# A decode block on one core: the q projection with a head's weights stationary, in a loop of 32 turns

## The chip, the cores and the metric

The kernel runs on one core of a Trainium2 chip. The metric is device time in microseconds (us), the median of repeated runs. A profile of one execution shows, for each engine, when each instruction ran and what released it. PE is the matrix engine (PEld its weight loads, PEq or PEldq the instructions of its sequencer: registers, branches), DVE the vector engine, ACT the scalar engine, POOL a fourth engine that only prepares constants here, and SP the engine whose queue issues nearly all DMA transfers.

## What is computed

One decode step of a transformer block for four sequences: layer norm, attention over a cache of 8192 positions with 32 heads of 128, output projection, residual, layer norm, a gated MLP, residual. All inputs are bf16.

```python
# x: 4 x 1 x 512; k_cache, v_cache: 4 x 32 x 8192 x 128; wq: 512 x 4096; wo: 4096 x 512
q = (layernorm(x) @ wq).reshape(B, Sq, H, Dh).transpose(0, 2, 1, 3)
scores = einsum("bhqd,bhkd->bhqk", q, k_cache) * (Dh ** -0.5)
o = einsum("bhqk,bhkd->bhqd", softmax(scores), v_cache)
h = x + o.transpose(0, 2, 1, 3).reshape(B, Sq, H * Dh) @ wo
g, u = layernorm(h) @ w_gate, layernorm(h) @ w_up       # 512 x 1792 each
return h + (sigmoid(g) * u) @ w_down
```

The query is one row for each sequence, so q is a product of a 4 x 512 matrix with a 512 x 4096 one: small work beside the caches, of which every byte is read once (some 537 MB of the 551 MB that the kernel reads).

## The kernel before

**Units.** The 4 x 32 pairs of sequence and head are worked in 32 units of 4 heads (`NU = 32`, `HU = 4`). A unit's K is one transfer of 8 MB into one of two slots of the tile `KV` (slot 0 for even units, slot 1 for odd), its V one of 8 MB into slot 2. The weights `wq` (4 MB) are loaded first, into slot 2 too, so V of unit 0 can't be issued before the q projection has read them.

**The DMA queue.** SP issues every large transfer in one fixed order: wq, then K0, K1, V0, K2, V1, K3, V2, and so on (lines 532 to 542; the list `order`, line 225). The first three go out at once. V0 waits for `t_qp`, the last product of the q projection (line 535). After that K of unit u waits for the last transposition of unit u-2 (`t_kd`, a small memset on DVE in line 361), and V of unit u waits for the product that reads the last of V of unit u-1 (`t_vd`, line 419). An issue that waits holds back all issues behind it on SP.

**A unit.** `unit(u)` emits, on PE and DVE: `scores(u)`, 16 chunks, for each a DVE block transposition of K (line 335) and four PE products against the queries (line 344; a loop of 8 turns on PE, two chunks a turn); `maxima(u)` on DVE and the exponential on ACT; the query tile of the next unit (`q_window`, line 328); `pv(u - 1)`, 64 products of the previous unit's weights with its V (line 405), the scaling copy on ACT (line 410) and four small products (line 415); and `weights(u)`, four DVE transpositions of the exponentials (line 375). Between units 1 and 31 PE runs one loop turn a unit, DVE and ACT one loop turn for two units.

**The q projection.** After the layer norm of x (lines 273 to 287), 32 products (line 301) run in two groups of 16, one for each half of the 4096 columns: the stationary operand is a column group of the normalised x (128 x 4), the moving one 512 columns of wq, four products side by side in the array. DVE turns each group's result by blocks (line 308), and a cast (line 309) picks the bf16 queries out of the turned tile `qt` into `q_all`. Then `q_window(0)` (line 328) makes unit 0's query tile, and only behind it on DVE stands the first transposition of K0.

```python
t_qp = emit("pe", f, [t_wq, t_xn, t_ps0, t_selc], incs=4)
...
w = t_qp if n == 2 else None          # n counts the transfers of K and V: n == 2 is V0
```

Of the kernel before, what the change touches and what calls it, by code (L numbers as in the profile page):

```python
# [18 lines left out]
class _Prog:  # L19
# [52 lines left out]
    def emit(self, eng, fn, waits=(), incs=1, ch=None):  # L72
        todo = self._waits(eng, waits)
        key = ch or eng
        tok = self.token(key, incs) if incs else None
        self._put(eng, todo, key, fn, incs, 1)
        return tok
# [41 lines left out]
def bass_sequential_preLN__mha_block_cached__glu_gated_glu__decode_kernel(  # L119
# [12 lines left out]
    B, _sq, D = A_x.shape  # L132
    _, H, S, DH = A_k_cache.shape
    F = B_w_gate.shape[1]
    assert DH == 128 and H == 32 and D == 512 and F % 128 == 0 and B == 4 and S == 8192
    NC = D // 128
    NFT = F // 128
    FG = F // 4
    HU = 4
    NU = B * H // HU  # L140
    R = S // 32
    SLOT = R * DH
    NSL = 3
# [10 lines left out]
    prog = _Prog({"p2d": "dve", "d2d": "dve", "a2d": "dve", "d2p": "pe", "a2p": "pe",  # L154
                  "d2a": "act", "p2a": "act",
                  "k0": "dve", "k1": "dve", "v2": "pe"})
    emit = prog.emit

    with ExitStack() as es:
        def SB(name, shape, dt):  # L160
            return es.enter_context(nc.sbuf_tensor(name, shape, dt))

        def raw(t):
            return t.tensor if hasattr(t, "tensor") else t

        kT = SB("kT", [128, 2 * TW], FP32)
# [3 lines left out]
        q_all = SB("q_all", [128, NU, 4], BF16)  # L170
        spare = SB("spare", [128, 24], FP32)
        KV = SB("KV", [128, NSL * SLOT], BF16)
# [21 lines left out]
        agg = kT[0:B, TW + 264:TW + 266]  # L194
        std = kT[0:B, TW + 268:TW + 270]
        xnT = hnT = kTb[:, 2 * (TW + 288):2 * (TW + 288) + NC * B]
        qt = kT[:, 0:4 * NU // B * 32]
        h_sb = kT[0:B, TW + 512:TW + 512 + D]

        def reg(slot, off, size):  # L200
            return KV[:, slot * SLOT + off:slot * SLOT + off + size]

        wq_v = reg(2, 0, NC * H * DH).rearrange("p (c f) -> p c f", c=NC)
        x_bf = reg(2, 24 * 1024, D)[0:B, :]
        wo_v = reg(1, 0, WOJ * D).rearrange("p (j f) -> p j f", j=WOJ)
        wg_v = reg(1, 16384, NC * F).rearrange("p (c f) -> p c f", c=NC)
        wu_v = reg(1, 16384 + NC * F, NC * F).rearrange("p (c f) -> p c f", c=NC)
        wd_v = reg(2, 0, NFT * D).rearrange("p (t f) -> p t f", t=NFT)
# [6 lines left out]
        PS = es.enter_context(nc.psum_tensor("PS", [128, 4096], FP32))  # L215
        bank = [PS[:, 512 * i:512 * (i + 1)] for i in range(8)]
        SBK, OBK, EX, XS, XO, QB, DN = 0, 1, 2, 3, 4, (5, 6), 7
# [10 lines left out]
        t_wq = prog.token("wq", 16)  # L228
# [22 lines left out]
        for j in range(4):  # L251
# [9 lines left out]
        t_selc = emit("pool", lambda e: e.affine_select(  # L261
            out=hw4, in_=hw4, compare_op=ALU.is_ge, fill=0.0, base=31,
            pattern=[[0, 8], [32, 4], [0, 4]], channel_multiplier=-1), [t0])
        emit("pool", lambda e: e.memset(part[:, :], 1.0))
        t_pool = emit("pool", lambda e: e.memset(PTz[:, :], 0.0))
        for b in (OBK, EX, *QB, DN):
            t_ps0 = emit("act", lambda e, b=b: e.activation(bank[b], bass.AP(raw(Lq), 0, [[528, 128], [0, 512]]), ACT.Copy), [t_lq0])

        def cols(t, c):
            return t[:, c:c + NC * (B - 1) + 1:NC]  # L270

        def layernorm(src, waits, dst):
            a = emit("dve", lambda e: e.bn_stats(bst, src), waits)
            a = emit("dve", lambda e: e.bn_aggr(agg, bst), [a])
            a = emit("act", lambda e: e.activation(std[:, 0:1], agg[:, 1:2], ACT.Sqrt, bias=eps[0:B, :]), [a, t_eps])
            a = emit("dve", lambda e: e.reciprocal(std[:, 1:2], std[:, 0:1]), [a])
            t_row = emit("dve", lambda e: e.tensor_scalar(
                row, src, agg[:, 0:1], std[:, 1:2], op0=ALU.subtract, op1=ALU.mult), [a])

            def f(e):  # L280
                ins = None
                for c in range(NC):
                    ins = e.matmul(cols(bank[XS], c), row[:, c:c + NC * 127 + 1:NC], ident[0:B, 0:B],
                                   start=(c == 0), stop=(c == NC - 1), skip_group_check=True)
                return ins
            a = emit("pe", f, [t_row, t_ident])
            return t_row, emit("dve", lambda e: e.tensor_copy(dst, bank[XS][:, 0:NC * B]), [a])
# [3 lines left out]
             [t_x, t_ident])  # L291
        _, t_xn = layernorm(x_bf, [t_x], xnT)

        t_qr = []
        for g in range(2):
            def f(e, g=g):
                made = []
                for c in range(NC):
                    for h in range(HU):
                        rhs = wq_v[:, c, 2048 * g:2048 * (g + 1)].rearrange("p (k h d) -> p h k d", k=4, h=HU)[:, h]  # L300
                        made.append(e.matmul(PS[32 * h:32 * h + B, 512 * QB[g]:512 * QB[g] + 512], cols(xnT, c), rhs,  # L301
                                             start=(c == 0), stop=(c == NC - 1), tile_position=(0, 32 * h)))
                return made[-4:]
            t_qp = emit("pe", f, [t_wq, t_xn, t_ps0, t_selc], incs=4)

            src = bank[QB[g]].rearrange("p (k w r) -> p r k w", k=8, r=2)
            dst = qt[:, 512 * g:512 * (g + 1)].rearrange("p (k r w) -> p r k w", k=8, r=2)
            t_qr.append(emit("dve", lambda e, src=src, dst=dst: e.transpose(dst, src), [t_qp]))
        t_q = emit("dve", lambda e: e.tensor_copy(
            q_all[:, :, :].rearrange("p (b g) t -> p g b t", b=B),  # L310
            qt.rearrange("p (g t w) -> p g w t", t=4, g=NU // B)[:, :, 0:B, :]), t_qr)

        t_tr, t_sc, t_pv, t_ex, t_mx, t_exp, t_ptz, t_lq, t_ocp, t_rs, t_kd, t_vd, t_sum = ({} for _ in range(13))
        TU = 2
# [107 lines left out]
        def unit(u, t=0):  # L422
# [6 lines left out]
            if u:  # L429
# [4 lines left out]
                                      skip_group_check=True), [t_pool, t_ps0], incs=0)  # L434
# [4 lines left out]
        for u in range(1, NU):  # L439
            t, first = divmod(u - 1, TU)  # L440
            if u == NU - 1:
                prog.close("dve", "act")
                t = 0
# [90 lines left out]
        for n, (x, u) in enumerate(order):  # L534
            w = t_qp if n == 2 else None
            if n >= 3:
                w = t_kd[u - 2] if x == "k" else t_kd[NU - 2] if u == NU - 1 else t_vd[u - 1]
            slot = slots[x, u]
            cache = A_v_cache if x == "v" else A_k_cache
            src = cache[u // (NU // B), HU * (u % (NU // B)):HU * (u % (NU // B) + 1), :, :].rearrange("h (p r) d -> (h p) (r d)", p=32)  # L540
# [51 lines left out]
```

## Time and profile before

| | us |
|---|---|
| median of three timed runs | 1277.33 (1277.13 to 1277.39) |
| span of the profiled execution | 1275.6 |
| what the timed median has over that span | 1.7 |
| PE busy, DVE busy, ACT busy in the span | 779.7, 762.3, 59.0 |
| the q projection on PE (line 301) | 13.00 to 16.59 |
| first transposition of K0 on DVE (line 335) | 32.27 |

The profiled execution has no time of its own beside its span; the span runs from its first instruction to its last, and the 1.7 us over it in the timed runs is what lies around. A row of the profile's timeline gives the start, the duration, the engine and line, what was written from what, and in brackets how long the engine had been idle before and what ended that. A chain that ended last is followed back from the last instruction; a row of it names who held up the end. Rows of PEldq are the sequencer's own instructions.

### The profile page before, as it was taken

What the parts mean: (1) busy time and instruction counts of PE and PEld (TensorE: products, weight loads), DVE (VectorE), ACT (ScalarE), POOL (GpSimd) and SP (SyncE); (2) the same over time, 40 slices, a digit from 0 to 9 for tenths busy, and PEclk for the clock granted to TensorE, in tenths of its full rate; (3) what the DMA queues carried; (4) which work ended last, traced back from release to release, by engine and by line L of the source; (5) the groups of instructions that cost most, each with busy time, mean ns of one, the idle gap of its engine ahead of it and who ended that gap; (6) DMA issues with size and microseconds to landing.
All of it is one profiled execution on the core that took longest, in us unless ns stands there. A gap on an engine that the chain in (4) does not pass through costs nothing.

```text
span 1275.6 us, 14073 instructions
## 1 busy us (share of the span) xinstructions
PE 779.7 (61%) x4588; PEld 328.5 (26%) x4636; DVE 762.3 (60%) x917; ACT 59.0 (5%) x114; POOL 5.7 (0%) x22
## 2 busy tenths in 40 slices
PE   1676755557755557655567655567555577555577
PEld 0232222223222223222222222222222232222233
DVE  1876665556665557665567655566655566655571
ACT  2000000000000000000000000000000000000001
POOL 1000000000000000000000000000000000000000
PEclk8888877788877788877788777788777888777888
DMA  9999999999999999999999999999999999999998
GB/s 423 432 426 430 427 450 434 430 430 427 454 430 430 430 427 454 432 427 430 430 452 432 427 430 434 450 430 427 430 440 444 430 427 430 442 442 430 430 427 371
DMA packets 10244, 550.83 MB, mean 432 GB/s; under 512 B 1144, under 2 KB 1152, under 8 KB 1408
## 3 DMA queue, kind: packets, MB, share of 16 engines
q1 hardware_dynamic: 10224, 550.77, 99.7%
q8 instruction: 2, 0.03, 0.0%
q10 hardware_dynamic: 16, 0.01, 0.0%
q14 instruction: 2, 0.02, 0.0%
HBM read 550.77 MB, written 0.00 MB: 432 GB/s over the span
## 4 chain that ended last, share of the span: by engine, by line
DMA 60%; PE 20%; DVE 12%; issue 2%; ACT 1%; SPq 0%; DVEq 0%
DMA KV<-in_A_k_cache_dram 58%; PE PS L344 14%; DVE kT L335 12%; PE PS L405 5%; DMA KV<-in_B_w_down_dram 3%; ACT kT L410 1%; PE PS L415 0%; SPq L541 0%; DVE PTz L375 0%; PE PS L521 0%; DVE KV L529 0%; SPq L557 0%; DVEq L112 0%
## 5 line engine op out<-in xcount | busy, mean ns | idle before, releaser
L344 PE MATMUL PS<-kT,Lq 128*128 128x512 bf16 x2048 | 588.7, 420 | 343.5 <-DVE kT L335 326.4
L335 DVE STREAM_TRANSPOSE kT<-KV 128x1024 f32<-128x1024 f32 x512 | 614.4, 1232 | 300.3 <-DMA KV<-in_A_k_cache_dram 237.5
L344 PEld LDWEIGHTS PS<-kT,Lq 128*128 x2048 | 210.3, 103 | 694.6 <-issue 621.7
L375 DVE STREAM_TRANSPOSE PTz<-E_sb 32x512 bf16<-32x512 bf16 x128 | 89.9, 703 | 129.1 <-PE PS L415 125.5
L405 PE MATMUL PS<-KV,PTz 128*16 128x512 bf16 x2048 | 117.0, 381 | 0.0
L379 PE MATMUL PS<-part,headw 128*128 128x2 f32 x64 | 18.8, 363 | 100.4 <-DVE PTz L375 100.4
L369 ACT ACTIVATE E_sb<-PS,negm 128x512 bf16<-128x512 f32 x32 | 22.0, 687 | 1139.4 <-DVE negm L367 1139.4
L405 PEld LDWEIGHTS PS<-KV,PTz 128*16 128x16 bf16 x2048 | 58.9, 111 | 56.3 <-issue 13.6
L415 PE MATMUL PS<-lane,kT 128*128 128x4 f32 x256 | 33.6, 255 | 31.0 <-ACT kT L410 31.0
L362 DVE TENSOR_REDUCE part<-PS 128x1 f32<-128x512 f32 x32 | 22.1, 691 | 38.7 <-PE PS L344 38.7
L415 PEld LDWEIGHTS PS<-lane,kT 128*128 128x128 f32 x256 | 31.0, 191 | 46.2 <-issue 44.8
L379 PEld LDWEIGHTS PS<-part,headw 128*128 128x128 f32 x64 | 16.0, 310 | 103.7 <-DVE PTz L375 103.7
L410 ACT ACTIVATE kT<-PS,rsb 128x512 f32<-128x512 f32 x32 | 22.0, 687 | 61.5 <-PE PS L405 61.5
L388 PE MATMUL PS<-Lq 128*128 128x512 bf16 x27 | 11.0, 462 | 2.9 <-issue 2.5
L328 DVE TENSOR_TENSOR Lq<-q_all,mask 128x32 bf16<-128x32 bf16 x32 | 9.5, 297 | 0.0
L454 DVE TENSOR_TENSOR kT<-PS,mask 128x512 bf16<-128x512 f32 x1 | 0.7, 692 | 13.3 <-PE PS L415 13.3
L367 DVE STREAM_TRANSPOSE negm<-mxr 128x32 f32<-128x32 f32 x32 | 6.8, 212 | 1.1
L364 DVE STREAM_TRANSPOSE turn<-part 128x32 f32<-128x32 f32 x32 | 6.8, 211 | 1.1
L388 PEld LDWEIGHTS PS<-Lq 128*128 128x128 bf16 x44 | 4.8, 116 | 8.3 <-issue 6.1
L322 PEld LDWEIGHTS PS<-Lq,headw 128*128 128x128 bf16 x32 | 3.5, 108 | 12.8 <-issue 11.3
L396 DVE RECIPROCAL rsb<-PS 128x1 f32<-128x1 f32 x32 | 6.3, 197 | 0.7 <-PE PS L379 0.7
L301 PE MATMUL PS<-KV,kT 128*4 128x512 bf16 x32 | 3.6, 627 | 5.0 <-DMA KV<-in_A_wq_dram 5.0
(70 smaller groups left out, 56.7 us busy)
## 6 DMA issues: line engine op xcount, KB each, us to landing
KV<-in_A_wq_dram SPq DMA_DIRECT2D x1, 4096.0 KB, 12.2
KV<-in_A_wo_dram SPq DMA_DIRECT2D x1, 4096.0 KB, 27.2
KV<-in_B_w_gate_dram SPq DMA_DIRECT2D x1, 1792.0 KB, 31.1
KV<-in_B_w_up_dram SPq DMA_DIRECT2D x1, 1792.0 KB, 34.9
KV<-in_B_w_down_dram SPq DMA_DIRECT2D x1, 1024.0 KB, 32.1
KV<-in_A_k_cache_dram SPq DMA_DIRECT2D x32, 49.6
KV<-in_A_v_cache_dram SPq DMA_DIRECT2D x32, 30.7
KV<-in_B_w_down_dram SPq DMA_DIRECT2D x1, 512.0 KB, 32.9
```

Of the source, the lines that this page charges most:

```text
L328: t_lq[u] = emit("dve", lambda e, ix: e.tensor_tensor(dst, bass.AP(raw(q_all), at(ix, 0) * (4 * TU) + 4 * (u - TU * t), [[NU * 4, 128], [1 ...
L335: t_tr[u, c] = emit("dve", lambda e: e.transpose(kT[:, (c % 2) * TW:(c % 2 + 1) * TW], KVw[:, o:o + TW]), w, ch="d2p")
L344: ins = e.matmul(bank[SBK], bass.AP(raw(Lq), ix[-1] * 2 + (128 * t + c % 2), [[528, 128], [1, 128]]), rhs, start=False, stop=False, skip_g ...
L362: a = emit("dve", lambda e: e.tensor_reduce(part[:, 0:1], bank[SBK], AX.X, ALU.max), [t_sc[u, NT - 1], t_pool], ch="d2d")
L364: a = emit("dve", lambda e: e.transpose(turn_[:, :], part[:, :]), [a], ch="d2d")
L369: t_exp[u] = emit("act", lambda e: e.activation(E_sb[:, :], bank[SBK], ACT.Exp, bias=negm[:, 0:1], scale=SCALE, accum_out=part[:, 1:2]), [ ...
L375: return [e.transpose(PTz[32 * q:32 * (q + 1), :].rearrange("p (r q c) -> p r q c", r=4, q=4)[:, :, q, :], E_sb[32 * q:32 * (q + 1), :].re ...
L379: t_sum[u] = emit("pe", lambda e: e.matmul(bank[QB[1]][:, 0:2], headw[:, :], part[:, 0:2], start=True, stop=True), [t_ptz[u], t_selc], ch= ...
L388: emit("pe", lambda e: [e.matmul(bank[XS], Lq[:, 0:128], Lq[:, 0:512], start=True, stop=True) for _ in range(n)][-1], [t_ps0, t_lq[NU - 1] ...
L405: made.append(e.matmul(PS[32 * j:32 * j + 16, ob:ob + 512], lhsT, KV[:, slot * SLOT + 512 * k:slot * SLOT + 512 * (k + 1)], start=(k < 4), ...
L410: t_ocp[u] = emit("act", lambda e: e.activation(O_sb, bank[OBK], ACT.Copy, scale=rsb[:, 0:1]), [t_pv[u], t_rs[u]], ch="a2p")
L415: ins = e.matmul(bass.AP(raw(PS), at(ix, 0) * 4 + (512 * EX + 4 * (u - t)), [[4096, 128], [1, 4]]), O_sb[:, 128 * q:128 * (q + 1)], lane[: ...
```

## The change

The weights of a head become the stationary operand (128 x 128) and x the moving one (128 x 4). A turn of the loop does the four products of one head, one for each group of 128 rows of wq; 32 turns do the 32 heads, and each head's result stands as four columns of one PSUM bank, already with the head's 128 dimensions on the partitions. Ahead of the loop and behind it stands one more product (`q_ends`): the first takes the waits, the last gives the signal `t_qp`; their result is not used. The block turns and the tile `qt` are gone; one cast reads PSUM and writes `q_all`.

```diff
-        for g in range(2):
-            def f(e, g=g):
-                made = []
-                for c in range(NC):
-                    for h in range(HU):
-                        rhs = wq_v[:, c, 2048 * g:2048 * (g + 1)].rearrange("p (k h d) -> p h k d", k=4, h=HU)[:, h]
-                        made.append(e.matmul(PS[32 * h:32 * h + B, 512 * QB[g]:512 * QB[g] + 512], cols(xnT, c), rhs,
-                                             start=(c == 0), stop=(c == NC - 1), tile_position=(0, 32 * h)))
-                return made[-4:]
-            t_qp = emit("pe", f, [t_wq, t_xn, t_ps0, t_selc], incs=4)
...
-            t_qr.append(emit("dve", lambda e, src=src, dst=dst: e.transpose(dst, src), [t_qp]))
+        def q_ends(waits):
+            return emit("pe", lambda e: e.matmul(bank[XS][:, 0:B], wq_v[:, 0, 0:128], cols(xnT, 0), start=True, stop=True),
+                        waits)
+
+        def q_head(e, ix):
+            for c in range(NC):
+                e.matmul(bass.AP(raw(PS), ix[0] * B + 512 * QB[0], [[4096, 128], [1, B]]),
+                         bass.AP(raw(KV), ix[0] * DH + (2 * SLOT + c * H * DH), [[NSL * SLOT, 128], [1, DH]]), cols(xnT, c),
+                         start=(c == 0), stop=(c == NC - 1), skip_group_check=True)
+
+        q_ends([t_wq, t_xn, t_ps0, t_selc])
+        prog.open("pe")
+        for _ in range(H):
+            prog.begin("pe")
+            emit("pe", q_head, incs=0)
+            prog.end("pe")
+        prog.close("pe")
+        t_qp = q_ends([])
         t_q = emit("dve", lambda e: e.tensor_copy(
-            q_all[:, :, :].rearrange("p (b g) t -> p g b t", b=B),
-            qt.rearrange("p (g t w) -> p g w t", t=4, g=NU // B)[:, :, 0:B, :]), t_qr)
+            q_all[:, :, :].rearrange("p (b g) t -> p g t b", b=B),
+            bank[QB[0]][:, 0:H * B].rearrange("p (g t b) -> p g t b", t=HU, b=B)), [t_qp])
```

All lines below the q projection move down by two (the transposition of K is line 337 in the changed kernel, the score products line 346).

PE, from its first instruction to the clearing product of unit 0, before; `KV` holds x and wq, `kT` the normalised x, and the last two rows stand behind the q projection:

```order
L290 MATMUL PS<-KV,ident 4x512
L283 MATMUL PS<-ident,kT 128x4 x4
L301 MATMUL PS<-KV,kT 4x512 x32
L433 MATMUL PS<-PTz 128x128
L322 MATMUL PS<-Lq,headw 128x512
```

PE in the changed kernel, one turn of the loop that stands in the place of the row of line 301. An ISA row sets registers (the address of the weights, and in the first one that of the result too); the turn adds to its counter and jumps back in the last two:

```order
L112 UNCONDITIONAL_BRANCH
L112 ISA
L299 ISA
L299 MATMUL PS<-kT,KV 128x4
L299 ISA
L299 MATMUL PS<-kT,KV 128x4
L299 ISA
L299 MATMUL PS<-kT,KV 128x4
L299 ISA
L299 MATMUL PS<-kT,KV 128x4
L112 REGISTER_ALU
L112 COMPARE_AND_BRANCH
```

What was 32 products without a register among them is now 32 turns of five register instructions, four products, an addition and a branch.

DVE at the same place, before: the layer norm, the q projection's turns and cast, the query tile of unit 0, the 16 transpositions of K0.

```order
L277 TENSOR_SCALAR kT<-KV,kT 4x512
L287 CAST kT<-PS 128x16
L308 STREAM_TRANSPOSE kT<-PS 128x2x8x32 x2
L309 CAST q_all<-kT 128x8x4x4
L328 TENSOR_TENSOR Lq<-q_all,mask 128x32
L335 STREAM_TRANSPOSE kT<-KV 128x1024 x16
```

And DVE in the changed kernel:

```order
L276 TENSOR_SCALAR kT<-KV,kT 4x512
L286 CAST kT<-PS 128x16
L311 CAST q_all<-PS 128x32x4
L330 TENSOR_TENSOR Lq<-q_all,mask 128x32
L337 STREAM_TRANSPOSE kT<-KV 128x1024 x16
```

The two block turns are gone; the cast still stands ahead of the query tile, and that ahead of the transpositions of K0. The order of the transfers on SP is as before, and so is the wait of V0 on `t_qp`.

More of the change, by code (lines that the diff above doesn't have):

```diff
@@ L196, in bass_sequential_preLN__mha_block_cached__glu_gated_glu__decode_kernel @@
         xnT = hnT = kTb[:, 2 * (TW + 288):2 * (TW + 288) + NC * B]
-        qt = kT[:, 0:4 * NU // B * 32]
         h_sb = kT[0:B, TW + 512:TW + 512 + D]
@@ L292, in bass_sequential_preLN__mha_block_cached__glu_gated_glu__decode_kernel @@
         _, t_xn = layernorm(x_bf, [t_x], xnT)
-        t_qr = []
-        for g in range(2):
-            def f(e, g=g):
-                made = []
-                for c in range(NC):
-                    for h in range(HU):
-                        rhs = wq_v[:, c, 2048 * g:2048 * (g + 1)].rearrange("p (k h d) -> p h k d", k=4, h=HU)[:, h]
-                        made.append(e.matmul(PS[32 * h:32 * h + B, 512 * QB[g]:512 * QB[g] + 512], cols(xnT, c), rhs,
-                                             start=(c == 0), stop=(c == NC - 1), tile_position=(0, 32 * h)))
-                return made[-4:]
-            t_qp = emit("pe", f, [t_wq, t_xn, t_ps0, t_selc], incs=4)
-            src = bank[QB[g]].rearrange("p (k w r) -> p r k w", k=8, r=2)
-            dst = qt[:, 512 * g:512 * (g + 1)].rearrange("p (k r w) -> p r k w", k=8, r=2)
-            t_qr.append(emit("dve", lambda e, src=src, dst=dst: e.transpose(dst, src), [t_qp]))
+        def q_ends(waits):
[14 more added lines that the diff above has]
+        t_qp = q_ends([])
         t_q = emit("dve", lambda e: e.tensor_copy(
-            q_all[:, :, :].rearrange("p (b g) t -> p g b t", b=B),
-            qt.rearrange("p (g t w) -> p g w t", t=4, g=NU // B)[:, :, 0:B, :]), t_qr)
+            q_all[:, :, :].rearrange("p (b g) t -> p g t b", b=B),
+            bank[QB[0]][:, 0:H * B].rearrange("p (g t b) -> p g t b", t=HU, b=B)), [t_qp])
         t_tr, t_sc, t_pv, t_ex, t_mx, t_exp, t_ptz, t_lq, t_ocp, t_rs, t_kd, t_vd, t_sum = ({} for _ in range(13))
```

## The prediction

> **What bounds the kernel now.** I read the page's span, DMA rows and chain first, then the timeline of the first 130 us, then the sequencer's instructions on PE.
>
> ```profile
> span 1275.6 us, 14073 instructions
> q1 hardware_dynamic: 10224, 550.77, 99.7%
> DMA 60%; PE 20%; DVE 12%; issue 2%; ACT 1%; SPq 0%; DVEq 0%
> ```
>
> The transfers take 99.7% of the span: the kernel ends when the last byte has come, so an edit costs only what it makes the DMA queue stand empty. The chain still has 20% PE and 12% DVE, since a transfer is issued when a slot comes free. The question is thus how much slack each issue has, and the first ones matter, since the change is at the start:
>
> ```profile
> 0.81 0.38 SPq L532 DMA_DIRECT2D KV<-in_A_wq_dram  x1
> 1.24 0.96 SPq L541 DMA_DIRECT2D KV<-in_A_k_cache_dram  x2
> 13.00 0.10 PEld L301 LDWEIGHTS PS<-KV,kT 128*4 128x4 bf16 x8 [5.12 <-DMA KV<-in_A_wq_dram]
> 13.00 3.59 PE L301 MATMUL PS<-KV,kT 128*4 128x512 bf16 x32 [5.04 <-DMA KV<-in_A_wq_dram]
> 16.71 0.33 SPq L541 DMA_DIRECT2D KV<-in_A_v_cache_dram  x1
> 16.72 0.72 DVE L308 STREAM_TRANSPOSE kT<-PS 128x512 f32<-128x512 f32 x1 [0.99 <-PE PS L301]
> 17.47 0.27 DVE L309 CAST q_all<-kT 128x128 bf16<-128x128 f32 x1
> 17.77 0.29 DVE L328 TENSOR_TENSOR Lq<-q_all,mask 128x32 bf16<-128x32 bf16 x1
> 32.27 2.37 DVE L335 STREAM_TRANSPOSE kT<-KV 128x1024 f32<-128x1024 f32 x2 [14.21 <-DMA KV<-in_A_k_cache_dram]
> 53.38 0.33 SPq L541 DMA_DIRECT2D KV<-in_A_k_cache_dram  x1
> 59.75 2.37 DVE L335 STREAM_TRANSPOSE kT<-KV 128x1024 f32<-128x1024 f32 x2
> 86.88 0.33 SPq L541 DMA_DIRECT2D KV<-in_A_v_cache_dram  x1
> 91.74 2.37 DVE L335 STREAM_TRANSPOSE kT<-KV 128x1024 f32<-128x1024 f32 x2 [1.21 <-DMA KV<-in_A_k_cache_dram]
> 119.32 0.33 SPq L541 DMA_DIRECT2D KV<-in_A_v_cache_dram  x1
> 130.35 2.37 DVE L335 STREAM_TRANSPOSE kT<-KV 128x1024 f32<-128x1024 f32 x2 [7.37 <-DMA KV<-in_A_k_cache_dram]
> ```
>
> The rows give: wq lands at 13.00; the projection is done at 16.59; the query tile of unit 0 at 18.06; then DVE waits 14.21 us for K0, which lands at 32.27. That is the cover of the q projection. Unit 0 runs from 32.27 to 59.75 (27.48 us), unit 1 follows without a gap although K1 had long landed (8 MB take 32.27 - 13.00 = 19.27 us, so K1 was there at 51.5), and V1 goes out at 86.88, 27.13 us into unit 1. At that moment K2 alone is left in the queue; it lands at 91.74. So V1 has 4.86 us to spare, less the time that an issue takes to bring data. In unit 2 the same gap is 130.35 - 119.32 = 11.03 us. The first two units, back to back with no V between K0 and K1, are the tightest place of the run: whatever delays the first transposition of K0 delays V1 by as much, and beyond some 3 us of it the queue runs dry.
>
> **What goes.** 32 products in 3.59 us, two turns of 0.72 and the cast of 0.27. Off the path today: 14.21 us of waiting stand behind them. Behind the last product stay one cast (0.30 from its start to the next, by line 309) and the query tile (0.29), 0.59 us where 1.34 stood (16.72 to 18.06).
>
> **What comes: the turn of the loop.** No row shows this loop, but two others show its parts, the score products (one register instruction for each product) and the filler loop of line 388 (two products a turn, no addresses):
>
> ```profile
> L344 PEldq FUSED_REGOPS  x4: 46/46/46, 52.0 to 52.4; - x4
> 52.14 0.34 PEld L344 LDWEIGHTS PS<-kT,Lq 128*128 x3 [0.59 <-issue]
> 51.00 0.39 PEld L344 LDWEIGHTS PS<-kT,Lq 128*128 x3 [0.77 <-issue]
> L344 PEld LDWEIGHTS PS<-kT,Lq x16: 95/96/97, 99.8 to 103.9; 128*128 x16
> L415 PEldq FUSED_REGOPS  x1: 60/60/60, 118.8 to 118.8; - x1
> L112 PEldq ALU_OP  x12: 36/36/36, 1243.9 to 1248.2; - x12
> L112 PEldq COMPARE_BRANCH  x12: 76/208/209, 1244.0 to 1248.3; - x12
> 7.67 0.29 PE L283 MATMUL PS<-ident,kT 4*128 4x4 bf16 x4 [4.66 <-DVE kT L277]
> 1257.98 0.27 PE L461 MATMUL PS<-laneb,kT 128*128 128x32 bf16 x4 [0.79 <-DVE kT L454]
> ```
>
> - *A product with its register instruction.* Three weight loads take 0.34 us from the first's start to the last's end, and one lasts 0.096: the step is (0.34 - 0.096) / 2 = 0.12 us; four register instructions from 52.0 to 52.4 agree. The register instruction is busy for 0.046 of it. I take 0.125. Upper bound (0.39 - 0.096) / 2 = 0.147, by the row at 51.00; lower bound 0.29 / 4 = 0.07, four products of the array without registers (line 283; line 461 has the same load of 128 columns, 0.27).
> - *The way back.* Twelve turns' additions start from 1243.9 to 1248.2, so 4.3 / 11 = 0.39 us a turn, of which the jump is 0.208 (0.076 for the one that falls through). The loads and products of such a turn are handed over almost for nothing (eight loads in 0.10 us at 13.00, though each lasts about that), so I take 0.37 for the way back.
> - *The turn's first register instruction* sets more registers than the others and no product stands behind it: between 0.046 and the 0.125 of a whole product, and, with the 0.060 of line 415 for its busy part, I take 0.11.
>
> A turn is 0.11 + 4 x 0.125 + 0.37 = 0.98 us. It is the sequencer's pace; the array needs 0.29 for four such products. 32 turns are 31.4, less 0.13 for the last jump: 31.2 us where 3.59 stood.
>
> **On the path.** The loop can't begin before wq is there, 13.00, plus 0.1 for its entry (an addition to a jump is about that): it ends at 44.3. The closing product (0.2, of 0.27 for four with their load) and its signal (0.13, from 16.59 to 16.72) bring the cast to 44.6, the cast and the tile the first transposition of K0 to 45.2, against 32.27: 12.9 us late, though K0 has landed. DVE is held in order behind the cast, and with it the 16 transpositions, then unit 0's maxima and unit 1. On SP, V0 waits for the closing product: 44.5, still 7 us ahead of the end of K1 at 51.5, so it costs nothing. K2 (53.38) goes to 66.3, and V0 ends at 51.5 + 19.3 = 70.8: 4.5 us of cover, still enough. V1 goes to 86.88 + 12.9 = 99.8, when K2 has landed 8 us ago. The queue is dry. What an issue needs until data lands has one small row:
>
> ```profile
> 0.80 0.57 ACTq L235 DMA_DIRECT2D KV<-in_A_x_dram  x1
> 2.41 0.68 DVE L273 BATCH_NORM_STATS2 kT<-KV 4x6 f32<-4x512 bf16 x1 [2.41 <-DMA KV<-in_A_x_dram]
> ```
>
> 4 KB take 1.6 us from issue to use. Bounds: 0, and 2.6, which is the 12.2 us from the issue of wq to its landing less half of 19.27 for its 4 MB. So V1 is late by 99.8 + 1.6 - 91.74 = 9.7 us, K3 behind it too, landing at 140.0. Unit 2 begins when unit 1 ends (91.74 - 1.21 = 90.53, now 103.4), and V2 goes out 27.58 us into it at 131.0, with 9 us to spare; from unit 3 on DVE waits for K again as it does now (7.37 us idle at 130.35). Nothing later gives the 9.7 us back, since the queue is full from there to the end.
>
> One gain is possible. Unit 0's chunks waited for a slow PE:
>
> ```profile
> 35.58 1.25 DVE L335 STREAM_TRANSPOSE kT<-KV 128x1024 f32<-128x1024 f32 x1 [0.94 <-PE PS L344]
> 37.29 13.58 DVE L335 STREAM_TRANSPOSE kT<-KV 128x1024 f32<-128x1024 f32 x11 [0.46 <-PE PS L344]
> 20.00:37.00 17.00, 3.34 (x8) 1.11 (x9) 3.62 (x3) 0.00 (x0) 0.00 (x0) 0.50 1.00 432
> 37.00:57.00 20.00, 14.67 (x57) 5.37 (x56) 17.23 (x21) 0.78 (x2) 0.00 (x0) 1.00 0.97 419
> ```
>
> The last two rows are sums over a stretch, with the granted clock third from the end: PE had half its clock from 20 to 37 us (0.50) and all of it from 37 on. If the loop wakes the clock ahead of unit 0, 0.94 + 0.46 = 1.4 us go. I take 0, as the array is idle for two thirds of each turn, and keep 1.4 for the range. The Trainium skill, "TensorE: Matmul & The Clock Gate", Part 1, holds that some 3.4 us of sustained activity open the clock. The rows agree: the score products that follow the transposition of 32.27 have it by 37. By that rule, if thin activity counts, the sum would be 8.3 us instead of 9.7.
>
> The sum: 1277.33 + 9.7 = 1287.0 us; the profiled span by the same step 1275.6 + 9.7 = 1285.3.
>
> **Rivals.**
>
> *The array sets the pace (the other side: not slower).* If register instructions run ahead while loads and products queue up, a head costs 0.29 us, 32 cost 9.3, the loop ends at 22.4, the tile is ready at 23.4, 8.9 us before K0: 1277.3. It decides at a turn of about 0.68 us: V1 has 4.86 - 1.6 = 3.3 us, so the first transposition may start at 35.5, the loop may end at 34.6 and last 21.5. For it: four products of this kind do follow each other at 0.07. Against it: the register instructions of line 344 step at 0.12 while the array could go faster, and the jump alone is 0.208 a turn. The same page of the Trainium skill, section "Back-to-back issue gap", gives a stream of loads and products with 128 columns about 81 ns each; 128 of them would take an estimated 10.4 us, and by that rule the time stays where it is; no run here shows such a stream. 9%, one of it for a gain that I don't see.
>
> *A cheap turn.* At 0.80 us (products at 0.09, way back 0.33) the loop takes 25.5, 5.7 less: 1281.3. It takes both near their lower ends. 6%.
>
> *Registers in the result's address.* Here the product itself has an address in a register, which line 344's has not. If that costs a second step like the load's, 0.07 more a product, the turn is 1.26, the loop 40.2, and V1 is later by 9.0: 1296.0. V0 would then go out at 53.5, after K1's end, but V1's lateness covers that. For it: nothing but the missing row. 6%.
>
> **How the numbers follow.** The forecast has 79%. Its own range: a turn between 0.90 and 1.07 (products at 0.147) is -2.6 and +2.9; the clock -1.4; the start of a dry queue -1.6 to +1.0. Not all ends meet: 1282.5 to 1291.0, which leaves out the first and last rival and the lower part of the second. A measurement can tell 0.2% from no change, 2.55 us: 1274.8 to 1279.9. Faster 1%, same 8%, slower 91%.
>
> **What would show it.** The loop of line 299 from 13.0 to 44 us, its register instructions in steps of 0.12 and a turn near 0.98; the cast of line 311 at 44 to 45, without a turn ahead of it; the first transposition of K0 (line 337) at 45, released by DVE's own cast and no more by K0; V1 issued near 99.8; DMA low for some 8 us from 92 on; K3 landing near 140; from unit 3 on the same rhythm, and the rest as now. Wrong: a loop that ends before 34 us, or V1 late with no gap in the DMA.

## The result, and the profile after

The changed kernel takes 1290.51 us (median of four runs, 1290.28 to 1292.74) beside 1277.23 for the kernel before: 13.3 us slower, a ratio of 1.0109 (95% interval 1.0098 to 1.0121). The direction and the way it comes about are as forecast; the size is not. 9.7 us were forecast, and the ratio, taken on the prediction's 1277.33, gives 1291.3, just over the top of the range (1291.0). The profiled execution is the run of 1292.74, with a span of 1291.5; the spans of the other three are 1289.0 to 1289.3. The 2 us that it has over those are lost behind the start of unit 31, in the last weights' transfers, so they are kept out of the comparison below, which goes by the start of unit 3.

The changed kernel's page, its span and its large transfers:

```profile
span 1291.5 us, 14540 instructions
q1 hardware_dynamic: 10224, 550.77, 98.6%
```

The same bytes, but the queue is no longer full. Its timeline at the q projection (start, duration, engine and line, idle time before and what ended it):

```profile
13.15 0.18 PE L294 MATMUL PS<-kT,KV 128*128 128x4 bf16 x1 [5.21 <-DMA KV<-in_A_wq_dram]
13.52 0.56 PE L299 MATMUL PS<-kT,KV 128*128 128x4 bf16 x4 [0.18 <-issue]
14.55 0.61 PE L299 MATMUL PS<-kT,KV 128*128 128x4 bf16 x4 [0.47 <-issue]
...
45.43 0.58 PE L299 MATMUL PS<-kT,KV 128*128 128x4 bf16 x4 [0.45 <-issue]
...
46.08 0.18 PE L294 MATMUL PS<-kT,KV 128*128 128x4 bf16 x1
...
46.30 0.33 SPq L543 DMA_DIRECT2D KV<-in_A_v_cache_dram  x1
46.30 0.71 DVE L311 CAST q_all<-PS 128x128 bf16<-128x128 f32 x1 [38.14 <-PE PS L294]
47.05 0.29 DVE L330 TENSOR_TENSOR Lq<-q_all,mask 128x32 bf16<-128x32 bf16 x1
47.16 2.36 DVE L337 STREAM_TRANSPOSE kT<-KV 128x1024 f32<-128x1024 f32 x2
...
48.54 1.89 PE L346 MATMUL PS<-kT,Lq 128*128 128x512 bf16 x4 [0.54 <-DVE kT L337]
```

Each turn shows four products and then 0.45 us in which PE waits for its own sequencer ("issue"). DVE, which waited 14.21 us for K0 before, now waits 38.14 us for the closing product, and the transposition of K0 begins at 47.16 without a wait for the DMA. The clock column of the windows (third from the end) reads 1.00 from the start of this execution on, and here behind the loop too:

```profile
46.00:52.00 6.00, 4.38 (x13) 1.42 (x12) 4.43 (x5) 0.00 (x0) 0.00 (x0) 1.00 1.19 513
```

That isn't the clock that PE had. The score products from 48.54 on start 0.43 us apart, the pace of unit 0 in the kernel before, where the column reads 0.50. The first clock record of this trace stands at 54.11, and the three products from 54.07 on start 0.22 to 0.24 apart. Ahead of its first record the column says nothing.

The sequencer's own rows in the loop (durations, then first and last start):

```profile
L112 PEldq COMPARE_BRANCH  x31: 215/215/232, 14.0 to 44.9; - x31
L112 PEldq FUSED_REGOPS  x30: 78/78/78, 14.3 to 44.2; - x30
L112 PEldq ALU_OP  x30: 36/36/36, 15.0 to 44.8; - x30
```

Thirty turns from the first jump to the last: (44.9 - 14.0) / 30 = 1.03 us. What this does further on:

```profile
68.65 0.33 SPq L543 DMA_DIRECT2D KV<-in_A_k_cache_dram  x1
...
75.02 2.37 DVE L337 STREAM_TRANSPOSE kT<-KV 128x1024 f32<-128x1024 f32 x2
...
102.53 0.33 SPq L543 DMA_DIRECT2D KV<-in_A_v_cache_dram  x1
...
106.22 2.37 DVE L337 STREAM_TRANSPOSE kT<-KV 128x1024 f32<-128x1024 f32 x2
...
133.49 0.33 SPq L543 DMA_DIRECT2D KV<-in_A_v_cache_dram  x1
...
143.84 2.37 DVE L337 STREAM_TRANSPOSE kT<-KV 128x1024 f32<-128x1024 f32 x2 [6.69 <-DMA KV<-in_A_k_cache_dram]
```

V1 goes out at 102.53 (86.88 before), and K3 lands at 143.84 (130.35 before): 13.49 us late. From there on DVE waits for K in each unit as it did, 6.69 us here, and nothing comes back. The gap itself stands in the windows of the changed kernel (the last two columns are the busy share of the DMA engines and GB/s; a packet is counted where it starts):

```profile
85.00:90.00 5.00, 4.23 (x18) 1.54 (x16) 4.82 (x5) 0.00 (x0) 0.00 (x0) 1.00 0.73 315
90.00:95.00 5.00, 4.23 (x17) 1.54 (x16) 4.81 (x5) 0.00 (x0) 0.00 (x0) 1.00 0.00 0
95.00:100.00 5.00, 4.61 (x57) 2.21 (x60) 2.93 (x10) 0.78 (x2) 0.00 (x0) 1.00 0.01 3
100.00:105.00 5.00, 2.20 (x32) 1.33 (x24) 1.66 (x3) 0.69 (x1) 0.00 (x0) 1.00 0.62 210
```

Ten microseconds of almost nothing, where the kernel before moved more than 400 GB/s. It is the only gap of that execution, from 90.70 to 103.51 by the packets, with one 16 KB block of instructions in it: 12.8 us.

### The profile page after: what moved, and what is told of

It is laid out like the page before. It is cut to its first block, busy times and chain, and to the rows that moved or that the text cites. A ratio compares the mean times of both kernels' runs of the same rounds, so it can differ in the third digit from the quotient of the medians.

```text
span 1291.5 us, 14540 instructions
## 1 busy us (share of the span) xinstructions
PE 817.9 (63%) x4734; PEld 342.1 (26%) x4734; DVE 761.6 (59%) x915; ACT 58.9 (5%) x114; POOL 5.7 (0%) x22
## 5 line engine op out<-in xcount | busy, mean ns | idle before, releaser
L417 PE MATMUL PS<-lane,kT 128*128 128x4 f32 x256 | 33.6, 255 | 31.0 <-ACT kT L412 31.0
L417 PEld LDWEIGHTS PS<-lane,kT 128*128 128x128 f32 x256 | 31.0, 191 | 46.2 <-issue 44.9
L299 PE MATMUL PS<-kT,KV 128*128 128x4 bf16 x128 | 18.2, 184 | 14.4 <-issue 14.4
L324 PE MATMUL PS<-Lq,headw 128*128 128x512 bf16 x32 | 18.7, 586 | 10.6 <-issue 9.6
L299 PEld LDWEIGHTS PS<-kT,KV 128*128 x128 | 13.3, 104 | 19.4 <-issue 17.0
L390 PE MATMUL PS<-Lq 128*128 128x512 bf16 x44 | 13.7, 479 | 0.2 <-issue 0.2
## 6 DMA issues: line engine op xcount, KB each, us to landing
KV<-in_B_w_down_dram SPq DMA_DIRECT2D x1, 1024.0 KB, 33.1
KV<-in_B_w_down_dram SPq DMA_DIRECT2D x1, 512.0 KB, 33.9
```

The costliest lines, as they stand in the source:

```text
L299: e.matmul(bass.AP(raw(PS), ix[0] * B + 512 * QB[0], [[4096, 128], [1, B]]), bass.AP(raw(KV), ix[0] * DH + (2 * SLOT + c * H * DH), [[NSL ...
L324: emit("pe", lambda e: e.matmul(bank[bk], headb, zeros, start=True, stop=False, skip_group_check=True), waits, incs=0)
L390: emit("pe", lambda e: [e.matmul(bank[XS], Lq[:, 0:128], Lq[:, 0:512], start=True, stop=True) for _ in range(n)][-1], [t_ps0, t_lq[NU - 1] ...
L417: ins = e.matmul(bass.AP(raw(PS), at(ix, 0) * 4 + (512 * EX + 4 * (u - t)), [[4096, 128], [1, 4]]), O_sb[:, 128 * q:128 * (q + 1)], lane[: ...
```

## The experiments

Theory A is the prediction's: the loop runs at the pace of PE's register instructions and jumps, so the queries are late, so the first transposition of K0 is late on DVE, so V1 is issued to an empty queue. The rivals: B, the form of the product costs (loads of 128 x 128, four columns moved); C, what costs is the late issue of V0, which also waits for the closing product; D, the loads take bandwidth from the transfers. The edits are to the changed kernel unless the text says otherwise.

**The products written out.**

```diff
-        prog.open("pe")
-        for _ in range(H):
-            prog.begin("pe")
-            emit("pe", q_head, incs=0)
-            prog.end("pe")
-        prog.close("pe")
+        for h in range(H):
+            emit("pe", lambda e, h=h: q_head(e, h), incs=0)
```

The addresses in `q_head` are then fixed ones.

> The change with its 128 products written out, all addresses fixed, no loop. Theory A (the loop's turns, paced by PE's register instructions and jump, hold back the queries, and with them the first transposition of K0 on DVE, until V1 is issued too late): without registers and jumps the products follow at 0.035 to 0.07 us, 4.5 to 9 us in all, the first transposition starts with the landing of K0 at 32.3, no gap in the DMA, 1277.2 us (within 1275 to 1279). Theory B (it is the form of the product that costs: loads of 128 x 128 weights out of the tile that the DMA writes, and four columns moved): the products stay near the 0.26 us each that they take in the loop, 33 us in all, and the time stays near 1290.

1278.39 us, a ratio of 1.0010 (1.0000 to 1.0019). PE in this kernel:

```profile
12.98 0.18 PE L294 MATMUL PS<-kT,KV 128*128 128x4 bf16 x1 [5.04 <-DMA KV<-in_A_wq_dram]
13.02 3.55 PE L299 MATMUL PS<-kT,KV 128*128 128x4 bf16 x128
16.44 0.17 PE L294 MATMUL PS<-kT,KV 128*128 128x4 bf16 x1
```

The same 128 products take 3.55 us, 0.028 each, where the loop needs 33. B falls: the form is as quick as the 32 products of before (3.59), and all of the rest is the loop. The DMA never stands still. The 1.3 us that stay are taken up further below.

**Two and four heads a turn.**

```diff
+            for h in range(2):
+                for c in range(NC):
+                    e.matmul(bass.AP(raw(PS), ix[0] * (2 * B) + (512 * QB[0] + h * B), [[4096, 128], [1, B]]),
+                             bass.AP(raw(KV), ix[0] * (2 * DH) + (2 * SLOT + c * H * DH + h * DH), [[NSL * SLOT, 128], [1, DH]]), cols(xnT, c),
...
-        for _ in range(H):
+        for _ in range(H // 2):
```

The kernel with four heads has 4 in the place of each 2.

> The change with two heads (eight products) a turn, 16 turns. Theory A: a turn of the change takes 1.03 us, of which four products with their register instructions are 0.50; with eight it is 1.53, 16 of them 24.5 us instead of 33.0. The first transposition of K0 goes from 47.16 to 38.7, and since it may start at about 33.5 (47.16 less the 13.67 us by which unit 4 and all later units are late in the changed kernel) before anything is lost, the time is 5.2 us over before: 1282.4 (1281 to 1284). Theory B: the same 128 products, 1290. Theory C (what costs is the late issue of V0, at 46.3 instead of 16.7): V0 goes out at 37.9, 30 us late before and now 21, so about two thirds of the loss stays, 1286.

> The change with four heads (16 products) a turn, 8 turns. Theory A: a turn is 1.03 + 3 x 0.50 = 2.53 us, 20.2 in all; the first transposition of K0 at 34.4, 0.9 us past the point from which it costs: 1278.1 (1277 to 1279.5), the queue dry for about a microsecond near 91 us or not at all. Theory B: 1290. Theory C: V0 at 33.6, 1284 or so.

Two heads: 1283.02 us, 1.0045 (1.0028 to 1.0061), the first transposition at 39.19. Four: 1279.22, 1.0017 (1.0007 to 1.0027), at 35.27. Both follow A within 1.2 us; B forecast 1290 for both, C 1286 and 1284. A turn takes 1.56 and 2.64 us, 0.03 and 0.11 more than forecast, since a head's products then need 0.54 us and not 0.50.

**The queries late, V0 on time**, in the kernel before:

```diff
+        t_late = t_qp
+        for _ in range(41):
+            t_late = emit("act", lambda e: e.activation(
+                bank[DN], bass.AP(raw(eps), 0, [[1, 128], [0, 512]]), ACT.Copy, scale=0.0), [t_late, t_eps])
         t_q = emit("dve", lambda e: e.tensor_copy(
...
-            qt.rearrange("p (g t w) -> p g w t", t=4, g=NU // B)[:, :, 0:B, :]), t_qr)
+            qt.rearrange("p (g t w) -> p g w t", t=4, g=NU // B)[:, :, 0:B, :]), [*t_qr, t_late])
```

> The kernel before, its q projection untouched and V0 issued at 16.7 as before, but the cast that makes the queries also waits for a chain of 41 copies on ACT, each waiting for the one ahead of it, that starts with the last product of the q projection and ends near 46 us (29 us at an estimated 0.7 each; the copies write zeros to a bank that is not used until the end). Theory A: only the first transposition of K0 counts; if it starts at T, the time is 1277.2 + (T - 33.5), so near 1290 for T near 46.5, with one gap in the DMA near 91 us. Theory C: V0 is on time, so 1277.2.

1286.17 us, 1.0067 (1.0050 to 1.0084). The copies took 0.63 us and not 0.7, so the queries came at 42.6. In this kernel:

```profile
12.88 3.59 PE L301 MATMUL PS<-KV,kT 128*4 128x512 bf16 x32 [4.93 <-DMA KV<-in_A_wq_dram]
...
16.59 0.33 SPq L545 DMA_DIRECT2D KV<-in_A_v_cache_dram  x1
...
42.57 0.27 DVE L313 CAST q_all<-kT 128x128 bf16<-128x128 f32 x1 [25.26 <-ACT PS L311]
42.87 0.29 DVE L332 TENSOR_TENSOR Lq<-q_all,mask 128x32 bf16<-128x32 bf16 x1
42.98 2.36 DVE L339 STREAM_TRANSPOSE kT<-KV 128x1024 f32<-128x1024 f32 x2
```

A gives 1277.2 + 42.98 - 33.5 = 1286.7 for that start, and 1286.2 came. The loss is there without the loop, without the new form, and with V0 at 16.59. C can't explain it.

**V0 late, the queries on time**, in the kernel before, with 47 such copies:

```diff
-            w = t_qp if n == 2 else None
+            w = t_late if n == 2 else None
```

> The kernel before, its queries and the first transposition of K0 on time, but V0 is issued only after a chain of 47 copies on ACT (0.63 us each by the run with 41 of them) that starts with the last product of the q projection: near 46.3 us, as in the changed kernel, instead of 16.7. Theory A (only the first transposition of K0 counts): K1 keeps the queue busy until 51.5, so V0 is still 5 us early; 1277.1 us, no gap in the DMA. Theory C (the late issue of V0 costs, alone or in part): up to 1290.

1276.96 us against 1276.96, 1.0001 (0.9991 to 1.0010):

```profile
32.50 2.37 DVE L339 STREAM_TRANSPOSE kT<-KV 128x1024 f32<-128x1024 f32 x2 [14.20 <-DMA KV<-in_A_k_cache_dram]
...
46.64 0.33 SPq L545 DMA_DIRECT2D KV<-in_A_v_cache_dram  x1
```

C has fallen. The two kernels take the change's two delays apart: the one for DVE costs all of it, the one for SP nothing.

**48 turns.**

```diff
         q_ends([t_wq, t_xn, t_ps0, t_selc])
+        prog.open("pe")
+        for _ in range(16):
+            prog.begin("pe")
+            emit("pe", q_head, incs=0)
+            prog.end("pe")
+        prog.close("pe")
         prog.open("pe")
```

> The change with 48 turns: a loop of 16 turns that makes the first 16 heads, and then the loop of 32 that makes them all once more. At 1.03 us a turn the first transposition of K0 goes from 47.2 to 63.7, and V0, which waits for the closing product, from 46.3 to 62.8, now behind the end of K1 at 51.5. Theory A: V1's issue sets the end, at one us for one us: 16.5 us more than the change, 1307. The DMA has two gaps, near 51 to 64 and near 104 to 121, together some 30 us. If the two lags add up instead (V0's 11 us on top), 1318. If the end of the queue were not what counts, no such slope.

1307.23 us, 1.0236 (1.0219 to 1.0253), the first transposition at 63.57. Here V0, at 62.71, is issued behind the end of K1, and the windows of this kernel show the two gaps:

```profile
50.00:55.00 5.00, 2.73 (x20) 1.96 (x19) 0.00 (x0) 0.00 (x0) 0.00 (x0) 1.00 0.00 0
55.00:60.00 5.00, 2.73 (x20) 1.98 (x20) 0.00 (x0) 0.00 (x0) 0.00 (x0) 1.00 0.00 0
...
105.00:110.00 5.00, 4.23 (x18) 1.54 (x16) 4.81 (x5) 0.00 (x0) 0.00 (x0) 1.00 0.00 0
110.00:115.00 5.00, 4.53 (x38) 1.80 (x40) 3.63 (x7) 0.00 (x0) 0.00 (x0) 1.00 0.02 3
```

A short third one of 1.8 us lies between them, since K2 goes out at 85.05, after V0 has landed. The total is what A has for V1's lateness alone: the gaps ahead of K2 move K2, and make the last one shorter by as much. The lags don't add up.

**The result's address fixed** (one register instruction less in each turn):

```diff
-                e.matmul(bass.AP(raw(PS), ix[0] * B + 512 * QB[0], [[4096, 128], [1, B]]),
+                e.matmul(bass.AP(raw(PS), 512 * QB[0], [[4096, 128], [1, B]]),
```

> The change with the result's address fixed: all heads write the same four columns, so the q of 31 heads is left out. A turn has four register instructions instead of five, the first one for counter and weights at once. Turn: 4 x 0.125 for products, 0.03 more for the longer first register instruction, 0.37 to 0.38 for the way back: 0.90 us instead of 1.03. Theory A: 32 x 0.13 = 4.1 us less, the first transposition at 43.0 instead of 47.2, 1286.4 us. If an address in a register costs in the product itself (the third rival of the prediction), more than that is saved: the products would follow at less than 0.12.

1286.77 us, 1.0076 (1.0059 to 1.0093), the first transposition at 43.05 (43.0 forecast). The sequencer's rows:

```profile
L112 PEldq FUSED_REGOPS  x31: 68/68/68, 14.0 to 41.2; - x31
L112 PEldq ALU_OP  x31: 36/36/36, 14.6 to 41.8; - x31
```

The turn is (41.8 - 14.6) / 30 = 0.91. It saves 0.12 us, the step of one register instruction, and no more: an address in the product's result costs only the instruction that makes it. The prediction's third rival falls with that.

**The cast in another order.**

```diff
-            q_all[:, :, :].rearrange("p (b g) t -> p g t b", b=B),
-            bank[QB[0]][:, 0:H * B].rearrange("p (g t b) -> p g t b", t=HU, b=B)), [t_qp])
+            q_all[:, :, :].rearrange("p (b g) t -> p b g t", b=B),
+            bank[QB[0]][:, 0:H * B].rearrange("p (g t b) -> p b g t", t=HU, b=B)), [t_qp])
```

> The change with the cast's loops in another order: written as in q_all, read from PSUM with a stride, instead of read in order and written with a stride of 1 KB between sequences. If the order of the writes is what makes it 0.71 us (0.27 before, for the same 128 x 128 values), it falls to about 0.3 and the first transposition of K0 starts 0.4 earlier, near 46.8. If it is the read from PSUM, it stays at 0.7 or grows. In the time 0.4 us can't be told.

One run, 1291.07 us, which tells nothing of 0.4. The row does:

```profile
46.08 0.29 DVE L311 CAST q_all<-PS 128x128 bf16<-128x128 f32 x1 [37.92 <-PE PS L294]
46.41 0.29 DVE L330 TENSOR_TENSOR Lq<-q_all,mask 128x32 bf16<-128x32 bf16 x1
46.52 2.36 DVE L337 STREAM_TRANSPOSE kT<-KV 128x1024 f32<-128x1024 f32 x2
```

It is the order of the writes: 0.29 us for the same values from the same bank, although the read now has the stride. (The stride that goes away is 64 bytes, 32 values of `q_all`, and not the 1 KB that the expectation names.)

**The products written out four times over**, and the simple form once more beside it:

```diff
-        for h in range(H):
+        for h in 4 * list(range(H)):
             emit("pe", lambda e, h=h: q_head(e, h), incs=0)
```

> The written-out form with its 128 products done four times over. By the first run with them written out they take 3.55 us, so 14.2 here: from 13.0 to 27.3, still under the landing of K0. Theory A: 1277.1 as before, and what the written-out form had over before (1.3 us in the median of ten runs, with K0's landing at 33.6 instead of 32.3) is chance or has another cause. Theory D (loading 128 columns of weights at this rate takes bandwidth of the tile from the transfers that write it): four times as long, so some 5 us over before, 1282, with K0 landing at 37 or so.

> The written-out form of the first batch once more, beside the fourfold one and with more rounds: whether its 1.3 us over before come again. Theory A: 1277.1 (1276.5 to 1278.5). Theory D: 1278.4, and K0 lands about 1.3 us later than in the kernel before.

The fourfold form took 1282.35 us, 1.0040 (1.0026 to 1.0054); the simple one 1277.86, 1.0009 (1.0000 to 1.0018). By the time alone, D would be right. The timeline of the fourfold form says why it isn't:

```profile
13.09 5.90 PE L299 MATMUL PS<-kT,KV 128*128 128x4 bf16 x216
21.86 3.57 PE L299 MATMUL PS<-kT,KV 128*128 128x4 bf16 x128 [2.87 <-issue]
29.15 3.57 PE L299 MATMUL PS<-kT,KV 128*128 128x4 bf16 x128 [3.73 <-issue]
36.45 1.23 PE L299 MATMUL PS<-kT,KV 128*128 128x4 bf16 x40 [3.72 <-issue]
...
38.60 2.37 DVE L332 STREAM_TRANSPOSE kT<-KV 128x1024 f32<-128x1024 f32 x2
```

The products keep their 0.028 us, but PE stops three times for 2.9 to 3.7 us, after 216 products and then twice after another 128, and the first transposition starts at 38.60. With that start A has 1277 + 38.6 - 33.5 = 1282.1, and the kernel keeps to it. K0's last packet lands at 33.1 (31.95 before), not near 37 as D has it. PE was waiting for instructions: between 13 and 45 us this execution has four transfers of the instruction queue, three of them one within each stop (19.48 to 20.36, 26.81 to 27.69, 34.08 to 35.01), where the kernel before has none. The Trainium skill, "Runtime: NRT & Kernel Launch", section "Instruction fetch mechanics", says that a sequencer fetches its program in blocks of 256 instructions. The trace agrees: 128 products with their loads are 256. The Trainium skill calls the cost at a block's edge mostly hidden; here it was 2.9 to 3.7 us, in a queue full of K.

The simple written-out form has one such transfer in that stretch, and in both of its executions K0 lands at 33.6 instead of 32.3. The packets show why. One DMA engine moves the block of 16 KB from 19.71 to 20.67, and from there its packets of K0 follow each other without a break to 33.20; the other fifteen have theirs by 31.95, as before. The second execution shows the same (19.68 to 20.65, then to 33.18). The loss of 0.9 to 1.3 us does not follow from A's rule, though: 33.6 is about where a loss begins, and by the table below it would cost 0.5 at most. In the first of the two executions the DMA engines were also idle for some 0.5 us in the mean, between 89 and 93; in the second they were not. The rest stays open.

**Eight heads a turn**, with the better cast:

```diff
+            for h in range(8):
...
-        for _ in range(H):
+        for _ in range(H // 8):
...
+            q_all[:, :, :].rearrange("p (b g) t -> p b g t", b=B),
```

> The change with eight heads (32 products) a turn, 4 turns, and the cast in the order of the run that had it 0.29 us long. Turns of 1.03, 1.56 and 2.64 us for one, two and four heads give 4.8 for eight, 19.2 in all; the loop ends near 32.4 and the first transposition of K0 starts near 33.2. Theory A: the runs so far lose one us for one us past 33.1 to 33.9, so nothing is lost here: 1276.9 to 1277.5, no gap in the DMA, the same as the kernel before; it can't be faster, since the queue was never empty there. Theory B (the form costs): well over 1278.

1277.08 us against 1276.89, 1.0002 (0.9993 to 1.0011):

```profile
32.49 0.29 DVE L312 CAST q_all<-PS 128x128 bf16<-128x128 f32 x1 [24.34 <-PE PS L294]
...
32.93 2.37 DVE L338 STREAM_TRANSPOSE kT<-KV 128x1024 f32<-128x1024 f32 x2
```

It is the time of the kernel before, with the loop, the stationary weights and the single cast in it. No version was faster than the kernel before, and none could be by this part, since the queue has no gap there to close.

All of them beside each other, T being the first transposition of K0 in the profiled execution and the loss the median over the kernel before's on the same chip:

| kernel | T, us | loss, us | T - loss |
|---|---|---|---|
| eight heads a turn | 32.93 | 0.2 | |
| four heads | 35.27 | 2.1 | 33.1 |
| written out, four times | 38.60 | 5.4 | 33.2 |
| two heads | 39.19 | 5.9 | 33.3 |
| queries late (no loop) | 42.98 | 9.1 | 33.9 |
| result's address fixed | 43.05 | 9.8 | 33.2 |
| the change | 47.16 | 13.3 | 33.9 |
| 48 turns | 63.57 | 30.3 | 33.3 |

Seven kernels that make the queries late in four different ways lie on one line: one us for one us, from 33.1 to 33.9. The simple written-out form (T 33.6, loss 0.9 to 1.3) does not.

T comes from one execution and the loss from whole runs, so the line looks a little tighter than it is. By the first transposition of unit 3 in the profiled executions, K3 is late by 0.8, 3.2, 4.3, 8.7, 8.6, 13.5 and 29.9 us, from four heads downwards. The slope is the same, but the line then begins between 33.7 and 35.4. The rest of the loss, up to 2.2 us, comes behind unit 3, part of it behind the start of unit 31; what makes it, no run shows.

## Why the prediction was right and where it fell short

The mechanism was right and its size was not. K3 was put 9.7 us late and was 13.5, since four terms were taken too small: the turn of the loop, the cast, the length of units 0 and 1, and the start of a dry queue.

- *What bounds the kernel, and that the first units are the tightest place*: right. One gap in the DMA, between K2 and V1; the same rhythm from unit 3 on.
- *The loop is paced by the sequencer, not the array*: right, and shown by the written-out form. A turn takes 1.03 us and not 0.98. By the starts of the sequencer's rows, in the mean over the loop, the four products with their register instructions take 0.51 (0.50 taken), the way back 0.38 (0.37), and the turn's first register instruction 0.14 (0.11). *That one was the most mis-sized of the three*: it is busy for 0.078 us where 0.060 was the longest seen. The 0.05 are 1.6 us over 32 turns: the closing product starts at 46.08, not 44.3.
- *The cast at 0.30*: wrong. It took 0.71, because it was priced by the cast of before without a look at its strides. 0.3 us of it reached the path, since the transposition starts 0.86 after the cast instead of 0.59.
- *12.9 us late*: 14.9 (47.16 - 32.27).
- *The slack*: taken too large. V1 followed 55.37 us after the first transposition instead of 54.61, since units 0 and 1 were each 0.38 us longer, with one more wait of DVE in each (0.46 us) for a PE at its slow clock; and the dry queue needed 2.7 us and not 1.6 (102.53 to 143.84 is 41.31, and two transfers in a full queue are 168.94 - 130.35 = 38.59, by the first transpositions of units 3 and 4 before). The bound of 2.6 from wq's own start was the right row: that, too, was a large transfer in an empty queue, and the row chosen was one of 4 KB. So 3.3 us of slack were reckoned with and 1.4 were there (14.9 less 13.5).
- *The sum*: 2.0 for the later start, 0.8 for the units, 1.1 for the dry queue make 9.7 into 13.5, which is K3's lateness (13.49). The errors all had one sign. The turn lay within its bounds, the dry queue's 2.7 just past its 2.6; the cast and the two units had been given no bound on the side to which they went.
- *V0 costs nothing*: right, by the kernel with V0 late. *K2's 4.5 us of cover are enough*: right, it goes out at 68.65 and the DMA is busy until 90.7.
- *The clock*: no gain, as forecast, but it had a cost that was put at nothing, the 0.8 us of units 0 and 1. The score products ran at the slow pace from 48.54 to 54.1, 5.6 us, where unit 0 of the kernel before had needed 3.5 (33.66 to 37.12); why it took longer is open. The loop ahead of them had kept PE busy for 0.56 of every 1.03 us, 33 us long, and had not opened the clock. The rule that the prediction takes from the Trainium skill, "TensorE: Matmul & The Clock Gate", Part 1, is that some 3.4 us of sustained activity open the clock; activity as thin as this did not count as sustained here.
- *The rivals*: the array's pace fell by the loop's rows, the cheap turn at 1.03, the registers in the result's address by the kernel with a fixed one.

## What to carry to other kernels

In a kernel that ends when its transfers end, ask of a step at the start how late it may be, follow that lateness to the first issue that it reaches, and compare it with what is still in the queue then: past that point each microsecond counts in full, before it none. A hardware loop has a price by the turn (here 0.52 us for the way back and the first register instruction, and 0.12 to 0.14 for each product with its address), so put more work into a turn until the step fits under what covers it; writing it all out has a price too, in instructions to be fetched through the same DMA. Price an operation by a row with its own strides and sizes, not by one with its name.

## What I had not expected

- 128 products with loads of 128 x 128 and four moved columns took 3.55 us, 0.028 each; 32 products of 512 columns had taken 3.59.
- A cast of 128 x 128 values from PSUM took 0.71 us when it wrote with a stride of 64 bytes in its innermost loop, and 0.29 when it wrote in the order of its tile and read with a stride instead.
- A program of 512 written-out products stopped three times for 2.9 to 3.7 us to fetch instructions, while transfers of 8 MB filled the queue.
- A loop that kept PE busy for half of each turn, 33 us long, did not open the clock.
- A single block of 16 KB of instructions on one of sixteen DMA engines made an 8 MB transfer land 1.3 us later.
- A queue that had run dry took 2.7 us more for the next two 8 MB transfers than a full one.
